# Layer one of two expert layers behind attention: 512-token first products beside attention, their results parked in DRAM, instead of 256-token products of both kinds with partial sums

## The chip, the cores and the metric

The kernel runs on one core of a Trainium2 chip. The metric is the device time of one execution in microseconds (us); three executions of the kernel before took 1135.73 to 1136.03, median 1135.93. Five engines work side by side: TensorE (PE in the profile; its weight loads are PEld), VectorE (DVE), ScalarE (ACT), GpSimd (POOL), and SyncE (SP), which here only issues DMA transfers. Each takes its own instructions in a fixed order and waits on semaphores for the others.

## The reference

Attention with a threshold per row, then two dense layers, each a product, a nonlinearity and a second product. All is float32.

```python
# 4 batches, 8 heads, 576 tokens, head size 64
scores = q @ k.T / 8
scores = where(scores >= max(scores) - tau, scores, -1e9)
x = softmax(scores) @ v            # -> x: 2304 tokens x 512
# layer one                         w_in: 512 x 2048, w_out: 2048 x 512
h = x @ w_in
g = where(h >= 1, h, where(h <= -1, 0, (h + 1)**2 / 4))
x2 = g @ w_out
# layer two, other weights
h = x2 @ w_in2
out = (h * clip(h + 3, 0, 6) / 6) @ w_out2
```

## The kernel before

**Dense layers.** Both are computed in a split form: each float32 operand is cut into a high part (type fp32r) and the remainder, and a product is the sum of three matmuls, high times high, high times low and low times high. Tokens lie along the free axis, in four main blocks of 512 (one a batch) and one block of 256 that collects the last 64 tokens of every batch. The 2048 inner columns are cut into 16 strips `f` of 128. `em_h` makes the first product of one strip: 4 slices of the inner 512 times 3 matmuls, 12 in all, into one PSUM bank; then ACT computes Relu and Square of it (L642, L643), DVE the rest of the nonlinearity (L644) into a tile `r`, ACT the high part `gh` (L650) and POOL the low part `gl` (L651). `em_out` adds a strip's second product to four accumulators, again 12 matmuls. The weights come as float64 words and are turned into high and low float32 parts by `split_a` and `split_b`, on ACT, DVE and POOL.

**Attention.** 16 jobs (`jobs`: a batch and a pair of heads), each of five blocks of queries. Per block: scores on PE (L296), negated copy and row minimum on DVE (L309), exponential on ACT (L320), mask and row sum on DVE (L328), turning by PE transposes (L254) that ACT copies out (`Gf`, L352), and the product with v (L388). One job after the other.

**How the two are put together.** While the first four jobs run there is nothing else for PE. From the fourth job on, `dense1` feeds pieces of layer one between the pieces of attention; `share` (0.57) says how much of it for each piece of attention. Its work is planned in `ROUNDS`: groups of 256 tokens (`GRP`) of the first three batches, and of the 16 strips only the first ten (`NF1`). A round makes ten first products (the first two groups in two halves of five), keeps the split results in SBUF, and makes the second products in two halves of the output rows in `em_part`, in one PSUM bank (Q3). The sum over these ten strips is a partial sum; it goes to the DRAM tile `x2p`. The first product has one PSUM bank while attention runs (`H_TAGS` is Q2 alone), the product with v has Q1, the transposes have Q0, and the scores have four banks in two pairs. After attention `dense` does the rest: batch 3 and the 256-token block in full, strips 10 to 15 of the first three batches (the partial sums are read back and added, L721), and then layer two.

**What sets the order.** The program is written step by step, but a scheduler places every instruction on its engine by a simulated timeline; `after` and `pin_mlp` add a few constraints. The order of each engine below is read from the built program.

```python
        credit = min(credit + share, 3.0)
        while credit > 0:
            c = next(part1)
            if c is None:
                break
            credit -= c
```

This loop runs once per piece of attention, and `part1` is `dense1`; it gives None when the next group's attention is not done.

## Time and profile before

| | |
|---|---|
| median of three executions | 1135.93 us (1135.73 to 1136.03) |
| span of the profiled execution, first to last instruction | 1136.9 us |
| PE busy | 1108.0 us, 97% of the span |
| DVE, ACT, POOL busy | 575.6, 632.6, 404.3 us (51%, 56%, 36%) |
| granted TensorE clock, mean | 0.997 |
| moved by DMA | 80.09 MB, mean 70 GB/s |

The profiled execution is known by its span alone, which is 0.97 us above the median of the three. Attention begins at the start of the span; the first dense matmul on PE starts at 108.7 us, the last of attention ends at 492.4 us. From there to the end PE does only dense work. Matmuls overlap in the pipeline, so that what one of them costs is the distance from its start to the next one's, and not its own duration. One float32 matmul of the program (scores, product with v) stands as two instructions in the trace.

### The profile page before, as it was taken

What the parts mean: (1) busy time and instruction counts of PE and PEld (TensorE: products, weight loads), DVE (VectorE), ACT (ScalarE), POOL (GpSimd) and SP (SyncE); (2) the same over time, 40 slices, a digit from 0 to 9 for tenths busy, and PEclk for the clock granted to TensorE, in tenths of its full rate; (3) what the DMA queues carried; (4) which work ended last, traced back from release to release, by engine and by line L of the source; (5) the groups of instructions that cost most, each with busy time, mean ns of one, the idle gap of its engine ahead of it and who ended that gap; (6) DMA issues with size and microseconds to landing.
All of it is one profiled execution on the core that took longest, in us unless ns stands there. A gap on an engine that the chain in (4) does not pass through costs nothing.

```text
span 1136.9 us, 18024 instructions
## 1 busy us (share of the span) xinstructions
PE 1108.0 (97%) x6680; PEld 901.2 (79%) x6680; DVE 575.6 (51%) x1272; ACT 632.6 (56%) x1239; POOL 404.3 (36%) x383
## 2 busy tenths in 40 slices
PE   7998899999999999999999999999999999999998
PEld 5665567778777788788889988888888888898886
DVE  5888887766565565445545756557511111121111
ACT  5787987866666666556566766645432222333222
POOL 0222676411111111136645765557622222222221
PEclk8999999999999999999999999999999999999999
DMA  6434335222111210015322344533110110010001
GB/s 161 106 77 102 109 108 151 63 81 71 47 49 32 53 43 13 11 34 167 98 75 93 117 143 150 184 111 111 38 42 1 32 38 1 10 38 1 19 1 38
DMA packets 105368, 80.09 MB, mean 70 GB/s; under 512 B 66368, under 2 KB 90176, under 8 KB 105280
## 3 DMA queue, kind: packets, MB, share of 16 engines
q1 hardware_dynamic: 103920, 78.64, 23.9%
q8 instruction: 53, 0.87, 0.3%
q10 hardware_dynamic: 1360, 0.30, 0.1%
q14 instruction: 35, 0.29, 0.1%
HBM read 61.60 MB, written 17.30 MB: 69 GB/s over the span
## 4 chain that ended last, share of the span: by engine, by line
PE 88%; ACT 4%; DVE 4%; issue 1%; DMA 1%; POOL 1%; ACTq 0%; SPq 0%; DVEq 0%
PE Q L633 34%; PE P L675 27%; PE Q L695 7%; PE P L296 7%; PE Q L388 6%; PE Q L254 5%; DVE p L309 2%; ACT e L320 1%; PE P L254 1%; DVE p L328 1%; ACT Gf L352 1%; PE P L426 0%; POOL w_c L135 0%; DMA w_raw<-in_moe_w_in_dram 0%; DVE xl L617 0%
## 5 line engine op out<-in xcount | busy, mean ns | idle before, releaser
L651 POOL TENSOR_TENSOR gl<-r,gh 128x512 fp32r<-128x512 f32 (+1 forms) x190 | 203.3, 1071 | 548.4 <-ACT gh L650 547.9
L633 PE MATMUL Q<-xh,wih 128*128 128x512 f32 (+1 forms) x760 | 263.2, 346 | 2.5 <-DVE r L644 2.5
L633 PE MATMUL Q<-xh,wil 128*128 128x512 f32 (+1 forms) x760 | 257.0, 338 | 0.0
L633 PE MATMUL Q<-xl,wih 128*128 128x512 f32 (+1 forms) x760 | 256.8, 338 | 0.0
L647 DVE SCALAR_TENSOR_TENSOR r<-r,Q 128x512 f32<-128x512 f32 (+1 forms) x80 | 50.7, 634 | 249.0 <-ACT r L646 248.9
L650 ACT ACTIVATE gh<-r 128x512 fp32r<-128x512 f32 (+1 forms) x190 | 99.8, 526 | 126.2 <-PE P L675 53.3
L633 PEld LDWEIGHTS Q<-xh,wih 128*128 128x128 f32 x760 | 143.9, 189 | 25.0 <-issue 4.8
L633 PEld LDWEIGHTS Q<-xl,wih 128*128 128x128 f32 x760 | 143.9, 189 | 15.7
L633 PEld LDWEIGHTS Q<-xh,wil 128*128 128x128 f32 x760 | 143.8, 189 | 15.2
L646 ACT ACTIVATE r<-Q,three 128x512 f32<-128x512 f32 (+1 forms) x80 | 51.4, 643 | 143.7 <-PE Q L633 140.6
L309 DVE TENSOR_SCALAR_CACHE_REDUCE p<-P 128x576 f32<-128x576 f32 x144 | 104.3, 754 | 50.2 <-PE Q L254 32.0
L328 DVE SCALAR_TENSOR_TENSOR p<-p,th,e 128x576 f32<-128x576 f32 x144 | 121.3, 860 | 15.7 <-ACT e L320 14.9
L644 DVE SCALAR_TENSOR_TENSOR r<-r,Q 128x256 f32<-128x256 f32 (+1 forms) x110 | 55.0, 500 | 135.1 <-ACT r L643 127.7
L320 ACT ACTIVATE e<-p,nm 128x576 f32<-128x576 f32 x144 | 109.1, 774 | 25.4 <-DVE p L309 24.3
L254 PE MATMUL Q<-ident,p 128*128 128x128 f32 x656 | 109.8, 283 | 11.3 <-ACT Gf L352 4.9
L675 PE MATMUL P<-woh,gh 128*128 128x512 f32 x288 | 112.0, 390 | 0.6 <-DVE ob L733 0.6
L675 PE MATMUL P<-wol,gh 128*128 128x512 f32 x288 | 112.3, 390 | 0.0
L254 PEld LDWEIGHTS Q<-ident,p 128*128 128x128 f32 x656 | 74.5, 141 | 46.3 <-ACT Gf L352 12.7
L675 PE MATMUL P<-woh,gl 128*128 128x512 f32 x288 | 111.0, 390 | 0.0
L296 PE MATMUL P<-kt,qt 64*128 64x288 f32 (+1 forms) x640 | 100.5, 433 | 6.0 <-DVE p L309 4.9
L135 POOL TENSOR_TENSOR w_c<-w_c,w_raw 128x512 int32<-128x512 int32 x64 | 88.6, 1384 | 39.1 <-DVE w_c L133 22.7
L352 ACT ACTIVATE Gf<-Q 128x512 f32<-128x512 f32 x128 | 74.9, 594 | 40.0 <-PE Q L254 39.2
(84 smaller groups left out, 1865.1 us busy)
## 6 DMA issues: line engine op xcount, KB each, us to landing
w_raw<-in_moe_w_in_dram SPq DMA_DIRECT2D x32, 512.0 KB, 4.1
w_raw<-in_moe_w_out_dram SPq DMA_DIRECT2D x32, 512.0 KB, 3.7
kn<-in_k_dram SPq DMA_DIRECT2D x32, 128.0 KB, 2.6
vn<-in_v_dram SPq DMA_DIRECT2D x32, 128.0 KB, 2.9
x2p<-ob SPq DMA_DIRECT2D x16, 256.0 KB, 2.2
x2d<-ob SPq DMA_DIRECT2D x16, 256.0 KB, 4.1
xst<-x2d SPq DMA_DIRECT2D x16, 256.0 KB, 3.3
out_dram<-ob SPq DMA_DIRECT2D x16, 256.0 KB, 2.2
```

Source lines behind the costliest of these rows:

```text
L135: x = G.tensor_tensor(out=c.bitcast(I32), in0=c.bitcast(I32), in1=r, op=ALU.add)
L254: x = T.transpose(out, in_, ident)
L296: mm = T.matmul(o, qt[j][r, c], kt[j][r, k0:k0 + HS], start=True, stop=True, skip_group_check=True)
L309: reads(V.tensor_scalar(out=p[:, x], in0=s[:, :, 0:HS], scalar1=-1.0, scalar2=3e38, op0=ALU.mult, op1=ALU.min, accum_out=nm[:, x:x + 1]), ...
L320: pins["S"] = S.activation(out=e, in_=p[:, x], func=ACTF.Exp, bias=nm[:, x:x + 1], scale=-1.0)
L328: V.scalar_tensor_tensor(out=p[:, x], in0=p[:, x], scalar=th[:, x:x + 1], in1=e, op0=ALU.is_le, op1=ALU.mult, accum_out=zt[j][:, z:z + 1])
L352: S.activation(out=f[:, h, :, d0:d0 + 128], in_=tm.rearrange("p (c n) -> p c n", c=4), func=ACTF.Copy)
L633: mm = T.matmul(h, l[:, kk * 128:(kk + 1) * 128], r, start=(x == 0), stop=(x == 3 * KD - 1))
L650: x = S.activation(out=gh, in_=r, func=ACTF.Copy)
L651: y = G.tensor_tensor(out=gl, in0=r, in1=f32(gh), op=ALU.subtract)
L675: T.matmul(a, l, r, start=(first and x == 0), stop=(last and x == 2))
L695: mm = T.matmul(o, l, r, start=(f == fs[0] and x == 0 and i == 0), stop=(f == fs[-1] and x == 2 and i == 1), skip_group_check=True)
```

## The change

Beside attention only first products are made, on 512 tokens at once, for all 16 strips of the first three batches (48 steps of `em_h`). The result `r` is not split there: it goes to DRAM (`gd`, one tile for each block and strip). The function `second` later reads it back with `load_g`, splits it (`split_g`; for odd strips of layer one DVE makes the low part in POOL's place), and makes the second products of a block over all 16 strips in one go, so that partial sums, `x2p`, `em_part`, `ROUNDS` and the rows of `dense` that add partial sums go away. The first products of batch 3 and of the 256-token block run between the second products of the first two blocks. All 16 strips of `w_in` and four of `w_out` are prepared beside attention (before: ten of each). The transposes of attention get a second PSUM bank, Q3, by turns with Q0. `share` is 0.27.

```diff
-    GRP = 256
-    NG = (NB - 1) * MAIN // GRP
-    NF1 = 10
+    NO = 4
...
+    wide = {"g": ctx.enter_context(tc.tile_pool(name="g2", bufs=1))}
+    gd = [[dram.tile([128, n], F32, name=f"gd{w}_{f}") for f in range(KF)] for w, n in enumerate(WIDE)]
...
-        tm = bank("Q0" if mode["mlp"] or mode["n"] % 2 else "Q2")
+        tm = bank("Q0" if mode["n"] % 2 else "Q3" if mode["mlp"] else "Q2")
...
+    def split_g(m, g, f, r):
+        n = WIDE[g]
+        gh = wide["g"].tile([128, n], F32R, tag="gh", name="gh", bufs=MLAG + 1)
+        gl = wide["g"].tile([128, n], F32R, tag="gl", name="gl", bufs=MLAG + 1)
+        x = S.activation(out=gh, in_=r, func=ACTF.Copy)
+        if m == 0 and f % 2:
+            V.tensor_tensor(out=gl, in0=r, in1=f32(gh), op=ALU.subtract)
+        else:
+            pins["G"] = G.tensor_tensor(out=gl, in0=r, in1=f32(gh), op=ALU.subtract)
+        pins["S"] = x
+        gs[m, g, f] = (gh, gl)
...
-        hp_, hb = (mt, HOLD) if key[2] == 1 else (wide["g"], MLAG + 1)
-        r = hp_.tile([128, n], F32, tag="r", name="r", bufs=2)
+        r = (wide["x"] if m else mt).tile([128, n], F32, tag="r", name="r", bufs=2 if m else 3)
         if m == 0:
             S.activation(out=r, in_=h, func=ACTF.Relu, scale=0.5, bias=half)
             S.activation(out=r, in_=r, func=ACTF.Square)
-            vlast = V.scalar_tensor_tensor(out=r, in0=r, scalar=1.0, in1=h, op0=ALU.min, op1=ALU.max)
+            V.scalar_tensor_tensor(out=r, in0=r, scalar=1.0, in1=h, op0=ALU.min, op1=ALU.max)
+            nc.sync.dma_start(out=gd[g][f], in_=r)
...
+    def load_g(g, f):
+        r = wide["g"].tile([128, WIDE[g]], F32, tag="gin", name="gin", bufs=3)
+        nc.sync.dma_start(out=r, in_=gd[g][f])
+        split_g(0, g, f, r)
...
-    def em_part(key, half, f):
-        gh, gl = gs[key, f] if half == 0 else gs.pop((key, f))
...
-    def dense1(ready, ahead):
-        for n, l in enumerate(steps[:n_h]):
...
-            for i, (r, half, f) in enumerate(l):
-                if i == 1:
-                    pace(n + 0.5)
-                yield from em_part(round_key(r), half, f)
-                yield 0.33
+    def dense1(ahead):
+        for n, (g, f) in enumerate((g, f) for g in range(NB - 1) for f in range(KF)):
+            if (0, g) not in xs:
+                while not ready(g):
                     yield None
+                split_x(0, g)
+            ahead(n)
+            if g == NB - 2 and f in (KF - 4, KF - 3):
+                load_g(0, f - KF + 4)
+            yield from em_h(0, g, f)
...
+    def second(seq, hseq, ahead):
+        for n, (g, f) in enumerate(seq):
+            if n + MLAG < len(seq):
+                load_g(*seq[n + MLAG])
+            ahead(n)
+            for i in range(KD):
+                em_out(0, g, f, i, fin_whole)
+            if n < len(hseq):
+                hg, hf = hseq[n]
+                split_x(0, hg)
...
+                for _ in em_h(0, hg, hf):
                     pass
...
-    weights.items += [(kind, 0, f) for kind, f in by_use]
+    weights.add(0, range(KF), "i")
+    weights.add(0, range(NO), "o")
...
-    share = 0.57
+    share = 0.27
     FIRST, RATE = 5, 0.85
...
-    order3 = [NB - 1, *range(NB - 2), NB, NB - 2]
-    dense(0, 2, seq2, fin_whole, ahead2, [(1, order3[0], 3)], rest)
+    FIRST_B = [g for g in range(NB + 1)]
+    seq = [(g, f) for g in FIRST_B for f in range(KF)]
+    hseq = [(g, f) for g in (NB - 1, NB) for f in range(KF)]
+    second(seq, hseq, ahead2)
+    dense2([*range(NB - 1), NB, NB - 1], ahead3)
```

In the built program the matmuls of 256 tokens fall from 2016 to 576, and those of 512 rise from 2448 to 3168.

PE in the middle of attention, from the end of one first product to the start of the next (P are score banks, Q_ with a transpose's `ident` the turning of `p`). Before:

```order
L633 MATMUL Q_3425<-xh,wil_1094 128x256
L296 MATMUL P_3517<-kt,qt 128x288
...
L254 MATMUL Q_3441<-ident,p 128x128 x4
L695 MATMUL Q_3477<-gh,woh_2387 128x256
...
L695 MATMUL Q_3477<-gh,wol_2484 128x256
L254 MATMUL Q_3486<-ident,p 128x128
L633 MATMUL Q_3501<-xh,wih_1344 128x256
```

And after, at a place that fifteen of the 48 steps resemble:

```order
L630 MATMUL Q_3600<-xh,wih_2163 128x512
...
L630 MATMUL Q_3600<-xh,wil_2164 128x512
L249 MATMUL Q_3719<-ident,p 128x128 x4
L291 MATMUL P_3728<-kt,qt 128x288
...
L249 MATMUL Q_3755<-ident,p 128x128
L249 MATMUL Q_3762<-ident,p 128x128 x4
L630 MATMUL Q_3689<-xh,wih_2226 128x512
```

The twelve matmuls of a second product that stood between the two first products are gone; nine transposes and four score matmuls are left there.

ACT at the same places (L642 and L638 are the Relu, L643 and L639 the Square of the first product). Before:

```order
L642 ACTIVATE r<-Q_3425,half 128x256
L643 ACTIVATE r<-r 128x256
L650 ACTIVATE gh<-r 128x256
L352 ACTIVATE Gf<-Q_3441 128x4x128
L320 ACTIVATE e<-p,nm 128x576
```

After:

```order
L638 ACTIVATE r<-Q_3600,half 128x512
L347 ACTIVATE Gf<-Q_3719 128x4x128
L639 ACTIVATE r<-r 128x512
L363 ACTIVATE Gt<-Q_3755 128x128
L347 ACTIVATE Gf<-Q_3762 128x4x128
L315 ACTIVATE e<-p,nm 128x576 x2
```

The copy of the high part has gone from here, and a copy of transposes stands between Relu and Square.

SP at the first steps of the dense work (`vn`, `qn`, `kn` are attention's inputs, `w_raw` the weights). Before:

```order
L434 DMA xd_76<-xu 128x512
L438 DMA xd_80<-xu 128x64
L97 DMA w_raw<-in_moe_w_out_dram 128x1024
L241 DMA vn_96<-in_v_dram 128x4x64 x2
L242 DMA vn_96<-in_v_dram 64x64
L94 DMA w_raw<-in_moe_w_in_dram 128x4x256
```

After:

```order
L431 DMA xd_79<-xu 128x512
L435 DMA xd_83<-xu 128x64
L89 DMA w_raw<-in_moe_w_in_dram 128x4x256
L641 DMA gd_0_89<-r 128x512
L650 DMA gin<-gd_0_89 128x512
L236 DMA vn_174<-in_v_dram 128x4x64 x2
L237 DMA vn_174<-in_v_dram 64x64
L89 DMA w_raw<-in_moe_w_in_dram 128x4x256
```

The store of a strip and, for the first six strips, its reading back stand ahead of loads of attention and of weights.

## Rows read from the trace of the kernel before

**Rows 1.** The page: busy time of engines, PE and clock in 40 slices, bytes.
```profile
PE 1108.0 (97%) x6680; PEld 901.2 (79%) x6680; DVE 575.6 (51%) x1272; ACT 632.6 (56%) x1239; POOL 404.3 (36%) x383
PE   7998899999999999999999999999999999999998
PEclk8999999999999999999999999999999999999999
GB/s 161 106 77 102 109 108 151 63 81 71 47 49 32 53 43 13 11 34 167 98 75 93 117 143 150 184 111 111 38 42 1 32 38 1 10 38 1 19 1 38
```

**Rows 2.** Stretches: us, busy time of each engine (instructions), clock, DMA share, GB/s.
```profile
20.00:120.00 100.00, 92.87 (x686) 60.87 (x686) 87.81 (x261) 82.53 (x171) 22.63 (x28) 1.00 0.40 107
124.00:200.00 76.00, 69.42 (x516) 52.77 (x516) 63.22 (x146) 62.04 (x135) 54.06 (x52) 1.00 0.48 135
200.00:260.00 60.00, 58.28 (x456) 47.37 (x455) 41.25 (x116) 45.75 (x98) 17.31 (x21) 1.00 0.25 67
260.00:487.00 227.00, 223.93 (x1747) 181.03 (x1746) 127.94 (x379) 144.10 (x314) 30.68 (x48) 1.00 0.16 41
...
700.00:725.00 25.00, 25.00 (x112) 20.72 (x111) 16.02 (x22) 15.68 (x27) 14.87 (x12) 1.00 0.56 177
```

**Rows 3.** The chain that ended last, by time: start us, us, what.
```profile
79.03 2.31 PE Q L388 x20
...
99.74 2.31 PE Q L388 x20
...
260.75 2.84 PE Q L388 x20
...
292.71 2.84 PE Q L388 x20
...
515.07 7.19 PE Q L695 x60
...
545.41 2.72 PE Q L633 x12
```

**Rows 4.** Groups of PE instructions by shape: count, busy us, mean ns, idle before, releasers.
```profile
L633 PE MATMUL Q<-xh,wih 128*128 128x256 f32 x368 | 110.4, 300 | 2.5 <-DVE r L644 2.5
L254 PE MATMUL Q<-ident,p 128*128 128x128 f32 x656 | 109.8, 283 | 11.3 <-ACT Gf L352 4.9 <-DVE p L328 3.2 <-ACT Gt L366 2.3
L695 PE MATMUL Q<-gh,woh 128*128 128x256 f32 x240 | 74.6, 311 | 0.5 <-ACT ob L706 0.5
```

**Rows 5.** Timeline, one hand-over of the first product's bank: start us, us, what.
```profile
342.99 0.28 PE L633 MATMUL Q<-xh,wil 128*128 128x256 f32 x1
...
343.37 0.47 ACT L642 ACTIVATE r<-Q,half 128x256 f32<-128x256 f32 x1 [0.19 <-PE Q L633]
...
343.88 0.42 ACT L643 ACTIVATE r<-r 128x256 f32<-128x256 f32 x1
...
344.40 0.42 DVE L644 SCALAR_TENSOR_TENSOR r<-r,Q 128x256 f32<-128x256 f32 x1 [2.67 <-ACT r L643]
```

**Rows 6.** Timeline, the same hand-over early, where it held PE.
```profile
137.99 0.28 PE L633 MATMUL Q<-xh,wil 128*128 128x256 f32 x1
...
143.25 0.41 DVE L644 SCALAR_TENSOR_TENSOR r<-r,Q 128x256 f32<-128x256 f32 x1
...
143.71 0.39 PE L633 MATMUL Q<-xh,wih 128*128 128x256 f32 x1 [0.41 <-DVE r L644]
```

**Rows 7.** Groups of the same steps at 512 tokens, and of copies, by shape.
```profile
L642 ACT ACTIVATE r<-Q,half 128x512 f32<-128x512 f32 x34 | 23.0, 680 | 8.8 <-POOL gl L651 3.4 <-PE Q L633 2.7 <-DMA x2p<-ob 2.3
L643 ACT ACTIVATE r<-r 128x512 f32<-128x512 f32 x34 | 21.2, 627 | 0.5
L644 DVE SCALAR_TENSOR_TENSOR r<-r,Q 128x512 f32<-128x512 f32 x34 | 23.2, 686 | 67.2 <-ACT r L643 60.8 <-DMA xst<-xd 6.4
L650 ACT ACTIVATE gh<-r 128x512 fp32r<-128x512 f32 x98 | 61.7, 631 | 92.8 <-PE P L675 47.7 <-DVE r L647 35.4 <-DVE r L644 9.6
L651 POOL TENSOR_TENSOR gl<-r,gh 128x512 fp32r<-128x512 f32 x98 | 130.6, 1333 | 270.4 <-ACT gh L650 270.1
L352 ACT ACTIVATE Gf<-Q 128x512 f32<-128x512 f32 x128 | 74.9, 594 | 40.0 <-PE Q L254 39.2
```

**Rows 8.** Timeline: five transposes and eight score instructions on PE.
```profile
334.04 0.71 PE L254 MATMUL P<-ident,qn 128*128 128x128 f32 x5
...
334.68 1.19 PE L296 MATMUL P<-kt,qt 64*64 64x288 f32 x8
```

**Rows 9.** DMA issues: out<-in, count, KB each, median us to landing.
```profile
x2p<-ob SPq DMA_DIRECT2D x16, 256.0 KB, 2.2
...
xst<-x2d SPq DMA_DIRECT2D x16, 256.0 KB, 3.3
...
pb<-x2p SPq DMA_DIRECT2D x12, 256.0 KB, 4.4
```

More of the change, by code (lines that the diff above doesn't have):

```diff
@@ L811, in dense, with dense2 @@
+    def dense2(order, ahead):
+        seq = [(g, f) for g in order for f in range(KF)]
         for n, (g, f) in enumerate(seq):
-            key = (m, g, ph)
-            split_x(key)
-            ahead(n, g, f)
-            for c in em_h(key, m, f):
-                pass
-            if rest is not None:
-                rest(n)
-            if m == 0 and g < NB - 1 and f == fs[g][-3]:
-                load_part(g)
-            kk = fs[g].index(f) + KD + 1 - len(fs[g])
+            split_x(1, g)
+            ahead(n)
+            for _ in em_h(1, g, f):
+                pass
+            kk = f + KD + 1 - KF
@@ L968, in ahead3 @@
-    def ahead3(n, g, f):
+    H_TAGS[:] = ["Q0", "Q1", "Q2", "Q3"]
+    wide["wo"] = ctx.enter_context(tc.tile_pool(name="wext", bufs=1))
+    wide["late"] = ctx.enter_context(tc.tile_pool(name="late", bufs=1))
+    weights.add(0, range(NO, KF), "o")
+    for c in part1:
+        weights.half()
+    weights.add(1, range(KF), "i")
+    weights.add(1, range(KF), "o")
+    split_x(0, NB - 1)
+    FIRST_B = [g for g in range(NB + 1)]
+    seq = [(g, f) for g in FIRST_B for f in range(KF)]
+    hseq = [(g, f) for g in (NB - 1, NB) for f in range(KF)]
@@ new lines, in enter_second, with ahead2, ahead3 @@
+    def enter_second():
+        mt_es.close()
+        wide["x"] = ctx.enter_context(tc.tile_pool(name="xs2", bufs=1, side="right"))
+    def ahead2(n):
+        limit = 2 * KF
+        if n >= KF:
+            limit += min(n - KF, KF)
+        if n < KF:
+            weights.upto(KF + n + 1)
+        for _ in range(2):
+            if weights.done < limit:
+                weights.half()
+        if n == len(seq) - 2:
+            split_x(1, 0)
+    second(seq, hseq, ahead2)
+    def ahead3(n):
```

278 lines of the change are left out of this document (71 added, 207 removed).

## The prediction

> **What bounds the kernel now.** The page comes first: PE is busy 97% of the span and the granted clock is at full speed in all slices but the first [rows 1]. Then the stretches, because one share for a whole program hides where an engine waits. From 260 to 487 us, attention with dense work beside it, PE is busy 223.93 of 227 us, while DVE has 56% and ACT 63%; from 700 to 725 us, dense work alone, PE has all 25 us [rows 2]. The losses are early: 6.6 us of 76 from 124 to 200 us and 1.7 of 60 after that, where POOL is busy 71% of the time with weights and DVE and ACT are over 80% [rows 2]. Before the dense work begins (20 to 120 us) DVE has 88% and sets the pace. So the kernel is PE's issue rate plus some 11 us of waiting beside attention (6.6, 1.7 and 3.1), and a change is worth what it takes off PE's sequence, less what it makes PE wait.
>
> How much a matmul costs is read from the chain: 60 matmuls of 256 tokens take 7.19 us, 119.8 ns each, and 12 of 512 tokens take 2.72 us, 226.7 ns each [rows 3]. Two of the narrow ones cost 239.6, so a pair costs 12.9 ns more than one wide one. A job of attention without dense work takes 20.7 us (from 79.03 to 99.74), one with it 32.0 (260.75 to 292.71) [rows 3]; 114 narrow matmuls of dense work stand in such a job, 13.7 us, so attention itself needs 18.3 us of PE.
>
> **The change, part by part.**
>
> *Fewer, wider matmuls.* Of the 1104 narrow first-product matmuls (three forms of 368, [rows 4]) 384 belong to the 256-token block and stay; 720 go, and so do all 720 of the narrow second products (three forms of 240). They are 1440 x 119.8 = 172.6 us. In their place stand 720 wide ones, 720 x 226.7 = 163.2 us. PE is the path in both places, so the saving counts in full: **-9.4 us**. The Trainium skill has a rule against this: "TensorE: Matmul & The Clock Gate", Part 1, gives a warm start-to-start of N / 2.4 GHz plus about 2.5 ns, which would be 109.2 and 215.8 ns, and the saving 1.9 us by it. The rows measure more fixed time than that for each of these matmuls, and the sum goes by the rows.
>
> *Work moved out from under attention.* Beside attention PE had 1321 narrow matmuls, 158 us; now it has 576 wide ones, 131 us. The rest runs later, where PE is already full, so this moves time and doesn't add any, provided that the shorter stretch is still PE's. Its 363 us (124 to 487) become about 336. DVE was busy 232 us there and ACT 252 [rows 2]. DVE's dense part stays nearly the same (58 x 0.42 us of L644 and some 25 us of splits and copies against 48 x 0.69 and fewer splits [rows 5, 7]); ACT loses about 18 us, since the high part of the result isn't made there any more. That gives DVE 69% and ACT 70% of the new stretch. They have room on the mean; what they cost is latency.
>
> *The hand-over of the first product's bank.* Beside attention this product still has the one bank Q2: the next may start only when DVE's last step has read it. At 256 tokens this took 1.83 us from the start of the last matmul (342.99) to the end of L644 (344.82) where nothing was in the way [rows 5]. At 512 the Relu is 0.21 longer, the Square 0.21, DVE's step 0.27 [rows 7], and the last matmul 0.11: 2.63 us, or 2.41 behind the matmul's own slot. The second product's 12 matmuls, which stood between two first ones and covered this, are gone. In the built order fifteen of the 48 hand-overs have too little PE work between: typically nine transposes and four scores, 9 x 0.11 + 1.19 + some switching = 2.3 us [rows 8]. And at most of these ACT has a copy of transposes (0.594, [rows 7]) or a like piece between Relu and Square. Adding, for each place, 2.41 plus what ACT's order has between, less PE's work between, the fifteen shortfalls sum to 9.6 us (0.2 to 1.0 each). The same sum over the old order is 4.4 us, and PE really waited 2.5 [rows 4]. Scaled like that the new wait is 5.5, in full it is 9.6; net of the 2.5 it is 3.0 to 7.1. I take the middle: **+5.0 us**.
>
> *A second bank for the transposes.* PE waited 4.9 us for copies of `Gf` and 2.3 for `Gt` [rows 4], all with one bank where dense work ran. With two by turns part of that goes. Also POOL makes no low parts beside attention, and weights come in a slower succession (15 items over some 18 longer steps), in the very stretch that lost 8.3 us. Bounds 0 and -8; I take **-3.0 us**, near the waits named in that stretch's rows.
>
> *A pause.* Three blocks of 16 steps use up attention's batches just as they finish. Once, before the third block, some 14 us of attention's PE work stands alone in the order. Alone, attention runs at 20.7 us a job where PE needs 18.3 [rows 3]: 14 x 2.4 / 18.3 = **+1.8 us**.
>
> *DRAM.* Sixty-four stores and loads of 256 KB and sixteen of 128 KB come, 32 transfers of partial sums go; at the densest that is 256 KB for 2.72 us of PE, 94 GB/s, where slices of 184 GB/s stand in the page [rows 1]. A load lands in 3.3 to 4.4 us [rows 9]; with 0.63 for the high and 1.33 for the low part [rows 7] that is 6.4 us, against two steps (5.4 us) by which `second` asks ahead, and three buffers that let SP issue earlier. On SP a strip's store waits for DVE, and the first six readings back wait for their own store to land (2.2 us, [rows 9]); behind them stand loads of `vn`, `qn` and weights, for which unit and weight steps would wait if they were late. These are asked for about a job ahead. Between 0 and +4; I take **+0.5 us**, for the changes of block in the later part too.
>
> *At no cost.* The additions of partial sums (L721) and their loads were hidden beside PE's full stretch. The twelve remaining strips of `w_out` and layer two's weights are prepared in steps of 4.2 to 5.4 us, under engines that had 60% of the time beside the same PE rate [rows 2].
>
> *Sum.* -9.4 + 5.0 - 3.0 + 1.8 + 0.5 = -5.1 us on a span of 1136.9: 1131.8. The median lies 0.97 below that span, so **1130.8 us**, 0.45% less.
>
> **The rivals.** A measurement of this kernel can tell about 0.2%, 2.3 us, from no change.
>
> *Even.* The hand-overs cost their full 7.1, the transposes' bank gives nothing back since DVE and ACT set their copies' time: -9.4 + 7.1 + 1.8 + 0.5 = 0, 1135.9. For it: ACT's order puts a copy into nearly each short place. Against it: the old order, read the same way, waited only 57% of what it showed.
>
> *Slower: the hand-over is late everywhere.* Early chains were far longer than the undisturbed one: 5.67 us from the last matmul to the end of L644 at 137.99, and PE held by it [rows 6]. Fifteen such chains from 111 to 202 us average 3.9 us. If the first 16 steps have this plus 0.8, their shortfalls sum to 14.7; the later ones, with 0.6 more than undisturbed, 5.5. Net of 2.5: -9.4 + 17.7 + 1.8 + 0.5 = +10.6, 1146.5. It decides from the point where waits of the first product for DVE's last step exceed some 14 us. Against it: those early chains were made by weights and POOL at 71%, both thinner now.
>
> *Slower: the round trip is on the path.* If each load is issued only two steps ahead and never earlier, 48 steps without first products lose up to 0.4 us each: +19 on the rest, 1150. Against it: three buffers, and a slot that is free long before.
>
> *Much faster.* The early 8 us go nearly whole and the hand-overs cost 1: -9.4 + 1 - 8 + 1.8 + 0.5 = -14.1, 1121.8.
>
> *The quoted rule.* With 1.9 in place of 9.4 saved, the rest as forecast: +2.4, 1138.3. The chain's rows speak against it.
>
> **How the numbers follow.** Forecast (its own range 1127 to 1134) 0.50; even 0.18; hand-over late 0.12; round trip 0.03; much faster 0.14; the rule 0.03. Faster by more than 0.2% (under 1133.7): 0.48 of the forecast and the much faster case, 0.62. Within: even and the forecast's edge, 0.20. Slower: 0.18. The range from 1122 to 1140 leaves out the two slow mechanisms and the edge of the fast one.
>
> **What would show it.** Right: twelve wide matmuls in 2.72 us everywhere; waits of the first product for DVE's last step of 5 to 10 us in all, at fifteen or so places, nearly all under 1 us; attention's last PE work near 468 us in place of 492; PE full from there on. Wrong: gaps on PE behind `gin` or `gl` after attention; jobs beside dense work at much over 30 us; waits for `qn`, `kn` or weights; or a wide matmul that costs more than 227 ns while stores to DRAM run.

## The result and the profile after

The changed kernel takes **1153.41 us** (median of 4 runs, 1151.0 to 1154.1) where the kernel before took 1135.98 beside it: ratio 1.0148, 95% interval 1.0134 to 1.0163. That is 1.5% slower; the forecast was 1130.8, 0.45% faster. The profiled execution took 1154.1 us, its span is 1152.3, so 15.4 us more than the span before.

The page of the changed kernel, answering to [rows 1]: busy time, PE and clock in 40 slices, bytes. A slice is 28.8 us.

```profile
PE 1109.4 (96%) x5960; PEld 862.5 (75%) x5960; DVE 568.0 (49%) x1234; ACT 606.5 (53%) x1117; POOL 351.6 (31%) x313
...
PE   7999998989999999999998899999999999999998
...
PEclk9999999989999999999999999999999999999999
...
DMA packets 118691, 105.43 MB, mean 91 GB/s; under 512 B 68176, under 2 KB 90192, under 8 KB 118608
```

PE has 720 matmuls fewer and is still busy for the same 1109 us, against 1108.0. The recorded end of a matmul is modelled and a wide one is longer, so this line alone doesn't say whether time was saved. The slices say where it went. Between its first and its last slice the kernel before has 8s for PE from 85 to 142 us only; the changed one has them at 173 to 202, at 230 to 259 and from 605 to 662 us, and PEclk has an 8 at 230 to 259.

Stretches of the changed kernel, answering to [rows 2]: us, busy time of each engine (instructions), clock, DMA share, GB/s.

```profile
124.00:200.00 76.00, 69.45 (x420) 46.63 (x422) 56.71 (x140) 59.80 (x116) 33.42 (x33) 1.00 0.49 146
200.00:260.00 60.00, 54.45 (x297) 37.19 (x295) 46.08 (x113) 43.02 (x82) 22.67 (x21) 0.91 0.34 101
260.00:470.00 210.00, 205.71 (x1267) 145.95 (x1264) 125.65 (x359) 133.45 (x255) 5.87 (x14) 1.00 0.23 69
625.00:650.00 25.00, 16.97 (x65) 12.86 (x64) 17.45 (x25) 15.07 (x31) 15.62 (x12) 0.86 0.71 231
700.00:725.00 25.00, 25.00 (x112) 20.68 (x112) 2.83 (x5) 5.47 (x9) 5.91 (x5) 1.00 0.27 80
```

Three things are to be seen. From 124 to 200 us PE waits as long as before (6.55 against 6.58), although POOL is busy 44% instead of 71%. From 200 to 260 it now waits 5.55 (1.72 before), at a mean granted clock of 0.91. And from 625 to 650 us, long after attention, PE has only 16.97 of 25 us at a clock of 0.86, while DVE is busy 70%. At 700 PE is full, and DVE, ACT and POOL have next to nothing to do: the work that was there before (DVE 16.02, POOL 14.87 of 25 us, [rows 2]) has been done earlier.

The chain of waits, answering to the last two lines of [rows 3]: start, us, what.

```profile
493.19 2.72 PE Q L630 x12
495.91 2.72 PE P L679 x12
```

PE's groups by shape, answering to [rows 4]: count, busy us, mean ns, idle before, releasers.

```profile
L630 PE MATMUL Q<-xh,wih 128*128 128x512 f32 x512 | 206.4, 403 | 4.4 <-DVE r L640 4.1 <-ACT xh L601 0.2
...
L679 PE MATMUL P<-wol,gh 128*128 128x512 f32 x288 | 112.5, 391 | 2.1 <-POOL wol L134 2.1
...
L249 PE MATMUL Q<-ident,p 128*128 128x128 f32 x656 | 103.9, 282 | 10.3 <-DVE p L323 5.4 <-ACT Gf L347 3.1 <-ACT Gt L363 0.9
...
L679 PE MATMUL Q<-gh,woh 128*128 128x512 f32 x64 | 21.2, 413 | 8.2 <-DVE r L640 5.5 <-ACT gh L613 2.7
```

The saving is there: 12 wide matmuls take 2.72 us, 226.7 ns each, while stores and loads run. The wait for the hand-over of bank Q2 beside attention is small: 4.1 us, where I had expected 5 to 10. The new waits are the last row's 8.2 us, one of them 5.5 us long, and 2.1 us for weights of layer two.

**Where 15.4 us went.** For every kernel below I read from all PE records when attention's last PE work ends, and take off attention's own PE work (16 jobs, my estimate of 293.8 us, the same for all, so that only differences between kernels count) and the dense matmuls issued by then at 119.8 or 226.7 ns. What is left is the *loss beside attention*, the start included; the same from there to the end of the span is the *loss behind*. *Waits* are the time without any PE record, from 106 us to attention's end and from there on; the last column is the time at which the clock records show half speed (1.2 of 2.4 GHz), to the end of dense work, with "(at 12)" or "(at 88)" where it lies before the dense work. From the two prices as printed the loss behind comes out 0.3 to 0.5 us higher in every row; its differences hold to 0.2 us.

| kernel | median us | span | attention's end | loss beside | loss behind | waits beside / behind | half clock, us |
|---|---|---|---|---|---|---|---|
| before | 1135.98 | 1136.9 | 492.4 | 40.3 | 5.8 | 14.6 / 0.6 | 6.8 (at 12) |
| changed | 1153.41 | 1152.3 | 475.3 | 49.3 | 21.7 | 16.9 / 11.4 | 3.4 + 6.8, 6.8 behind |
| e1_late_w2 | 1150.11 | 1148.2 | 476.8 | 50.9 | 16.1 | 16.9 / 7.2 | 3.4 (at 12), 3.4 + 3.4 + 6.8 |
| e2_gin_late | 1152.56 | 1145.7 | 469.9 | 44.0 | 20.4 | 16.0 / 10.5 | 6.8 behind |
| e5_late_gin | 1148.40 | 1143.0 | 470.5 | 44.5 | 17.2 | 15.2 / 8.0 | 3.4 |
| e6_no_w2 | 1139.15 | 1136.3 | 473.1 | 47.2 | 7.9 | 16.4 / 1.8 | 3.4 + 3.4 |
| e10_low_on_dve | 1149.27 | 1150.5 | 476.5 | 50.5 | 18.7 | 17.9 / 7.6 | 3.4 (at 12), 3.4 + 6.8, 6.8 behind |
| e11_late_low_on_dve | 1142.64 | 1140.5 | 473.9 | 47.9 | 11.2 | 16.0 / 3.9 | 3.4 (at 88), 3.4 + 3.4 |
| e13_five_strips | 1130.02 | 1126.2 | 463.9 | 37.9 | 7.0 | 10.7 / 1.5 | none |
| e14_before_five_strips | 1131.24 | 1129.7 | 485.8 | 33.8 | 5.3 | 7.4 / 0.6 | 3.4 (at 88) |

The changed kernel against the one before: -9.4 for the matmuls, +9.0 beside attention (forecast +3.8), +15.9 behind it (forecast +0.5); sum +15.5. That this meets the spans' difference follows from how the losses are made and is no test of the -9.4.

**What stops PE at 626.9.** The timeline of the changed kernel; weight-load rows and other rows that aren't needed are left out. L119, L122 and L128 are DVE's three steps of a weight strip, L130 POOL's first; L111 and L118 are ACT's steps of a strip, L613 is ACT's high part of a result read back and L617 POOL's low part of one; L638 is the Relu of the first product, L639 its Square and L640 DVE's last step of it.

```profile
626.65 0.28 PE L630 MATMUL Q<-xh,wil 128*128 128x256 f32 x1
627.08 0.67 ACT L118 ACTIVATE w_c<-w_raw 128x512 f32<-128x512 f32 x1 [0.42 <-DMA w_raw<-in_moe_w_in_dram]
...
627.44 0.41 DVE L122 TENSOR_SCALAR w_c<-w_c 128x512 uint32<-128x512 uint32 x1
...
627.65 0.61 ACT L613 ACTIVATE gh<-gin 128x512 fp32r<-128x512 f32 x1
627.89 0.69 DVE L128 SCALAR_TENSOR_TENSOR w_c<-w_raw,w_c 128x512 uint32<-128x512 uint32 x1
628.17 0.66 ACT L111 ACTIVATE w_raw<-w_raw 128x512 int32<-128x512 uint32 x1
628.50 0.42 DVE L119 TENSOR_SCALAR w_c<-w_c 128x512 f32<-128x512 f32 x1
628.72 1.34 POOL L130 TENSOR_TENSOR w_c<-w_c,w_raw 128x512 int32<-128x512 int32 x1 [1.81 <-issue]
628.73 0.45 ACT L638 ACTIVATE r<-Q,half 128x256 f32<-128x256 f32 x1
628.95 1.39 DVE L122 TENSOR_SCALAR w_c<-w_c 128x512 uint32<-128x512 uint32 x1
629.22 0.42 ACT L639 ACTIVATE r<-r 128x256 f32<-128x256 f32 x1
630.02 1.45 POOL L617 TENSOR_TENSOR gl<-gin,gh 128x512 fp32r<-128x512 f32 x1
...
630.38 1.64 DVE L128 SCALAR_TENSOR_TENSOR w_c<-w_raw,w_c 128x512 uint32<-128x512 uint32 x1
...
631.94 0.41 DVE L640 SCALAR_TENSOR_TENSOR r<-r,Q 128x256 f32<-128x256 f32 x1
...
632.40 0.80 PE L679 MATMUL Q<-gh,woh 128*128 128x512 f32 x1 [5.47 <-DVE r L640]
```

PE has finished a narrow first product and comes to the next block of the second one, whose sums stand in banks Q0 to Q3. One of these is still to be read by L640. ACT is late first: it does L118, L613 and L111 before the Relu, which starts 1.80 us after PE's last matmul has ended (626.93). The Square ends at 629.64, and L640 starts 2.30 us later. In between stands DVE, which does steps of two weight strips first, 0.41, 0.69, 0.42, 1.39 and 1.64 us, and the last two take over twice what the same steps take at 627: each lies beside a POOL instruction. L640 itself, beside POOL too, takes its usual 0.41. PE waits 5.47 us, and towards the end of the wait the clock falls, to 1.2 GHz for 6.8 us from 631.4 on: 0.86 is the mean of this stretch.

### The profile page after: what moved, and what is told of

Its sections match the earlier page's. It is cut to its first block, busy times and chain, and to the rows that moved or that the text cites. A ratio compares the mean times of both kernels' runs of the same rounds, so it can differ in the third digit from the quotient of the medians.

```text
span 1152.3 us, 16662 instructions
## 1 busy us (share of the span) xinstructions
PE 1109.4 (96%) x5960; PEld 862.5 (75%) x5960; DVE 568.0 (49%) x1234; ACT 606.5 (53%) x1117; POOL 351.6 (31%) x313
## 4 chain that ended last, share of the span: by engine, by line
PE 74%; DVE 9%; ACT 6%; issue 4%; DMA 3%; POOL 3%; SPq 0%; ACTq 0%; POOLq 0%; DVEq 0%
PE Q L630 31%; PE P L679 23%; PE Q L385 6%; PE P L291 5%; PE Q L679 4%; PE Q L249 4%; DVE p L304 2%; DVE w_c L128 2%; DVE p L323 2%; DVE w_c L122 1%; POOL w_c L130 1%; DMA gin<-gd 1%; DMA gd<-r 1%; DVE w_c L119 1%; ACT e L315 1%
## 5 line engine op out<-in xcount | busy, mean ns | idle before, releaser
L630 PE MATMUL Q<-xh,wih 128*128 128x512 f32 (+1 forms) x640 | 242.5, 379 | 4.4 <-DVE r L640 4.1
L630 PE MATMUL Q<-xl,wih 128*128 128x512 f32 (+1 forms) x640 | 237.4, 371 | 0.0
L630 PE MATMUL Q<-xh,wil 128*128 128x512 f32 (+1 forms) x640 | 237.4, 371 | 0.0
L644 DVE SCALAR_TENSOR_TENSOR r<-r,Q 128x512 f32<-128x512 f32 (+1 forms) x80 | 50.7, 635 | 260.4 <-ACT r L643 260.3
L617 POOL TENSOR_TENSOR gl<-r,gh 128x512 fp32r<-128x512 f32 (+1 forms) x80 | 96.5, 1207 | 240.2 <-ACT gh L613 239.3
L630 PEld LDWEIGHTS Q<-xh,wih 128*128 128x128 f32 x640 | 121.5, 190 | 34.8 <-DVE r L640 9.0
L630 PEld LDWEIGHTS Q<-xl,wih 128*128 128x128 f32 x640 | 121.7, 190 | 21.3 <-DVE p L304 0.5
L630 PEld LDWEIGHTS Q<-xh,wil 128*128 128x128 f32 x640 | 121.3, 190 | 21.3
L643 ACT ACTIVATE r<-Q,three 128x512 f32<-128x512 f32 (+1 forms) x80 | 51.4, 644 | 149.2 <-PE Q L630 143.7
L323 DVE SCALAR_TENSOR_TENSOR p<-p,th,e 128x576 f32<-128x576 f32 x144 | 120.2, 859 | 9.3 <-ACT e L315 8.3
L304 DVE TENSOR_SCALAR_CACHE_REDUCE p<-P 128x576 f32<-128x576 f32 x144 | 104.5, 753 | 30.0 <-PE P L291 29.4
L249 PE MATMUL Q<-ident,p 128*128 128x128 f32 x656 | 103.9, 282 | 10.3 <-DVE p L323 5.4
L130 POOL TENSOR_TENSOR w_c<-w_c,w_raw 128x512 int32<-128x512 int32 x64 | 91.7, 1434 | 71.8 <-DVE w_c L128 31.0
L291 PE MATMUL P<-kt,qt 64*128 64x288 f32 (+1 forms) x640 | 98.8, 427 | 10.2 <-DVE p L304 7.0
L640 DVE SCALAR_TENSOR_TENSOR r<-r,Q 128x512 f32<-128x512 f32 (+1 forms) x80 | 50.4, 631 | 110.5 <-ACT r L639 110.4
L638 ACT ACTIVATE r<-Q,half 128x512 f32<-128x512 f32 (+1 forms) x80 | 51.1, 639 | 73.4 <-PE Q L630 73.2
L613 ACT ACTIVATE gh<-gin 128x512 fp32r<-128x512 f32 (+1 forms) x80 | 46.7, 585 | 73.3 <-PE P L679 37.5
```

The source lines that it names most:

```text
L130: x = G.tensor_tensor(out=c.bitcast(I32), in0=c.bitcast(I32), in1=r, op=ALU.add)
L249: x = T.transpose(out, in_, ident)
L291: mm = T.matmul(o, qt[j][r, c], kt[j][r, k0:k0 + HS], start=True, stop=True, skip_group_check=True)
L304: reads(V.tensor_scalar(out=p[:, x], in0=s[:, :, 0:HS], scalar1=-1.0, scalar2=3e38, op0=ALU.mult, op1=ALU.min, accum_out=nm[:, x:x + 1]), ...
L323: V.scalar_tensor_tensor(out=p[:, x], in0=p[:, x], scalar=th[:, x:x + 1], in1=e, op0=ALU.is_le, op1=ALU.mult, accum_out=zt[j][:, z:z + 1])
L617: pins["G"] = G.tensor_tensor(out=gl, in0=r, in1=f32(gh), op=ALU.subtract)
```

## The experiments

All run beside the kernel before, whose median was 1137.1 for e1 to e4, 1136.55 for e5 to e8, 1136.93 for e10 to e12 and 1137.3 for e13 to e15. Experiments e1 to e4 came first: two moves of work, two banks.

**e1_late_w2.** Layer two's first strips later and at half the pace:
```
-        if n >= KF:
-            limit += min(n - KF, KF)
+        if n >= 2 * KF:
+            limit += min((n - 2 * KF) // 2 + 1, KF)
```


> The changed kernel with layer two's 16 strips of w_in prepared one for every two steps from step 32 of the second products on, in place of one a step in steps 16 to 31 (beside the 256-token block). Theory W (those weights, on DVE and POOL in short steps, hold DVE's last step of the first products, and that holds PE at 632 us for 5.5 us, then in half clock): the wait at about 632 us and the half clock behind it go, the stretch after attention shrinks from 677 to about 664 us, the time from 1153 to about 1141. Theory D (the reading back from DRAM is late, whatever the weights do): the waits stay, 1150 or more. The stretch up to the end of attention stays at 475 us in both.

1150.11 us, ratio 1.0112 (1.0097 to 1.0127); loss behind 16.1 in place of 21.7. Waits of PE from 600 us on, in all and the longest:

```profile
PE Q L679 <- DVE gl L615: 2.7, 4, 1.4
PE P L679 <- POOL wol L134: 2.1, 2, 1.7
PE Q L679 <- ACT gh L613: 0.9, 1, 0.9
```

The wait of 5.5 us is gone, with the dip of the clock behind it; smaller ones for `gl` came in its place, since the strips now run beside steps of 2.72 us. The move takes back 5.6 of the 15.9 us that the loss behind had grown by, and 3.3 us of the median, where 12 were expected.

**e2_gin_late.** The first six readings back wait for the store of strip 11 of the third block:
```
-            nc.sync.dma_start(out=gd[g][f], in_=r)
+            x = nc.sync.dma_start(out=gd[g][f], in_=r)
+            if (g, f) == (NB - 2, KF - 5):
+                pins["D"] = x
...
-        nc.sync.dma_start(out=r, in_=gd[g][f])
+        x = nc.sync.dma_start(out=r, in_=gd[g][f])
+        after(x, pins["D"])
```


> The changed kernel with the first readings back held behind the store of strip 11 of the third block on SP, so that none stands between attention's loads early. Theory S (six readings back that wait on SP for their own store, 9 us of SP's time from 100 to 300 us, and their splits make the early dense stretch slow): attention ends 4 to 6 us before 475, the time falls to about 1148. Theory H (what is lost beside attention comes from the longer hand-over of the first product and from DVE slowed beside POOL, not from SP): attention ends at 474 to 476 and the time stays within 2 us of the changed kernel.

1152.56 us (1147.44 to 1154.74), ratio 1.0145 (1.0128 to 1.0162). The profiled execution is the fastest of its four; in it attention ends at 469.9 and no dip of the clock lies beside attention. Over all runs the gain can't be told from none. Together with e1 (e5) it may be 1.7 us.

**e3_two_h_banks.** Two banks for the first product beside attention, and one for the transposes as in the kernel before:
```
-        tm = bank("Q0" if mode["n"] % 2 else "Q3" if mode["mlp"] else "Q2")
+        tm = bank("Q0" if mode["mlp"] or mode["n"] % 2 else "Q2")
...
-    H_TAGS = ["Q2"]
+    H_TAGS = ["Q2", "Q3"]
```


> The changed kernel with two banks for the first product beside attention (Q2 and Q3), and one for attention's transposes as before the change. Theory Q (the single bank's longer hand-over is a main loss beside attention): waits of the first product for DVE's last step (4.1 us directly) go, attention ends 4 to 8 us before 475, and the time is about 1147. Theory H2 (DVE standing in its own order for that last step, 83 us of idle time from 100 to 475, is the loss, and a second bank doesn't shorten that): little changes, or the lost second bank of the transposes costs up to 3 us.

1176.64 us, ratio 1.0350 (1.0335 to 1.0366). PE's transposes by shape in it:

```profile
L249 PE MATMUL Q<-ident,p 128*128 128x128 f32 x656 | 111.0, 285 | 26.0 <-ACT Gf L347 18.1 <-DVE p L323 3.2 <-ACT Gf L350 2.5
```

The transposes wait 26.0 us in place of 10.3. So a second bank for the product, at this price, isn't what the changed kernel lacks beside attention. The exchange of the bank costs 23 us, but not by the bank alone: the scheduler also put 604 of the 3744 dense matmuls at other places among attention's.

**e4_p_banks.** The sums of the block that follows the narrow first products stand in P banks, so that L640 no longer holds them:
```
-            if m == 0 and g % 2 == 0 and g >= NB - 2:
+            if m == 0 and g == NB:
```


> The changed kernel with the accumulators of the third block's second product in the two score pairs (P) and not in the first products' four banks. Theory B (the 5.5 us wait is only the clash over these banks; the rest of the work is in time): the wait at 632 goes, the half clock with it, and the time is 8 to 11 us less, about 1143. Theory W (DVE, POOL and ACT are behind by then, whichever bank is used): PE stops nearby for the split of a strip read back (gh, gl), and the gain is under 4 us.

1160.06 us, ratio 1.0206 (1.0188 to 1.0223). Waits of PE from 600 us on:

```profile
PE P L679 <- DVE ob L690: 8.5, 2, 7.8
PE P L679 <- ACT ob L688: 4.2, 4, 2.1
```

The P banks were held as well: L690 and L688 copy out the sums of the block before, and L690 stands in the same late queue of DVE. Which bank PE meets decides where it waits; this run doesn't show a free one.

**e5_late_gin.** Both edits of e1 and e2.

> The changed kernel with two edits together: layer two's first strips are prepared at half the pace from the 33rd step of the second product on, and the first six readings back wait for the store of strip 11 of the third block. Theory W+S (layer two's strips beside the short steps cost DVE its time, about 6 us of the 16 by this edit; readings back in front of the loads on SP cost some 5 us beside attention): the two add, span 1141 to 1144, attention's last PE work near 470, loss behind it near 16. Rival R (each is only where the same late work shows, so that one takes what the other gave): no better than the first edit alone, 1148 to 1150.

1148.40 us (1141.7 to 1151.44), ratio 1.0094 (1.0068 to 1.012). The profiled span, 1143.0, is as expected, but three of six runs lie at 1151, and the median is the rival's: the gain beside attention doesn't hold in all runs. The runs at 1151 have a mean granted clock of 0.993 to 0.994, the faster three 0.998 to 1.000.

**e6_no_w2.** Layer two's strips left out; layer two takes layer one's:
```
-    weights.add(1, range(KF), "i")
-    weights.add(1, range(KF), "o")
...
-        wh, wl = wsp["i", m, f]
+        wh, wl = wsp["i", 0, f]
...
-        wh, wl = wsp["o", m, f]
+        wh, wl = wsp["o", 0, f]
```


> The changed kernel with nothing of layer two's weights loaded or prepared: layer two multiplies by layer one's split weights. So 32 strips of ACT, DVE and POOL work and 16.8 MB of loads are left out, and PE's work is the same. Theory W (the strips are what makes DVE late behind attention): the loss behind attention falls from 21.7 to 6 to 8 us, no wait of PE for DVE's last step at 632, no half clock there; span 1137 to 1139. Rival D (the round trip through DRAM, and the steps that ask only two ahead, cost it by themselves): the waits for gh and gin stay, the loss stays over 14, span over 1145. Beside attention nothing changes by either: its last PE work near 475.

1139.15 us (11 runs), ratio 1.0021 (1.001 to 1.0033), and loss behind 7.9. The stretch of it that answers to 625:650 above:

```profile
625.00:650.00 25.00, 23.74 (x103) 18.97 (x103) 10.40 (x14) 11.38 (x21) 5.34 (x4) 1.00 0.64 199
```

PE has 23.74 in place of 16.97 us at the full clock, with the same stores and loads of results. So 14.3 of the 17.4 us lost are the strips of layer two; the round trip by itself isn't it. Their loads go here together with their preparation, and no run leaves out the one without the other. That it is the preparation which holds PE at 626.9 is read from the timeline above.

**e7_spread_wo.** The four `w_out` strips beside attention spread out:
```
-        goal = min(2 * len(weights.items), 2 * FIRST + 2 * RATE * n)
+        goal = min(2 * len(weights.items), 2 * FIRST + 2 * RATE * n, 2 * KF + max(0, (n - 14) // 3))
```


> The changed kernel with the four strips of w_out beside attention spread: half a strip in three steps instead of 1.7 halves in each, since nothing needs them before attention ends. Theory B (two strips at once made DVE late for the softmax at 248 us, 2.13 us, and the clock fell behind it): no wait over 1.5 us and no half clock from 235 to 260, attention ends 3 to 6 us earlier, near 470; median near 1149. Rival (the strips are in any case too few, what is late is DVE behind ACT's Square): attention ends within 2 us of 475 and a dip of the clock comes elsewhere; median within 2 us of 1153.

1153.01 us, ratio 1.0144 (1.0129 to 1.0159). The dip from 249 us is gone from its profile, another stands at 181, and attention's end isn't earlier (476.4; by then 12 more dense matmuls are done, and the loss beside is 47.7). A miss: these four strips are at most a small part of what costs.

**e8_all_moved.** e5, e7, and three of layer two's `w_out` strips from the 66th step on:
```
+        if n >= 4 * KF + 2:
+            limit += (n - 4 * KF - 2) // 5 + 1
```


> All moves of work together: late readings back, w_out's strips spread beside attention, layer two's w_in at half the pace from the 33rd step, and three of layer two's w_out strips from the 66th step on (they are what layer two's second product waits for at 791 and 801). If the losses are those that the traces name, and they add: loss beside attention near the forecast's (attention ends near 468), behind it near 13, span 1136 to 1139, about the kernel before. If each move only makes other work late: 1146 to 1150.

1148.62 us, ratio 1.0097 (1.0084 to 1.011): no better than e5, so moving strips about gained nothing more.

**e10_low_on_dve.** POOL's low parts of strips and of layer one's results, behind attention, on DVE:
```
-        if m == 0 and f % 2:
+        if m == 0:
             V.tensor_tensor(out=gl, in0=r, in1=f32(gh), op=ALU.subtract)
...
-        x = G.tensor_tensor(out=lo, in0=f32(c), in1=f32(hi), op=ALU.subtract)
+        x = (G if mode["att"] else V).tensor_tensor(out=lo, in0=f32(c), in1=f32(hi), op=ALU.subtract)
```


> The changed kernel with POOL's two low parts behind attention given to DVE: that of the result read back (gl, every second one was on POOL) and that of a weight strip (L134). POOL keeps one piece a strip (L130). DVE then has some 70 pieces more. Theory P (DVE is late because each of its pieces that runs beside a POOL piece takes 1.4 to 1.8 us where it takes 0.42 to 0.69 alone, so the strips hurt by POOL and not by their number): DVE's L119, L122, L128, L615 fall to means under 0.75, the loss behind attention falls from 21.7 to 12 or less though DVE has more to do; median 1141 to 1146. Rival N (DVE has simply too many pieces and waits in its order): 70 pieces of 0.69 more, 48 us, make it worse; loss over 22, median 1154 or more.

1149.27 us, ratio 1.0111 (1.0096 to 1.0125). DVE's groups from 470 to 800 us in it; the same lines in the changed kernel have means of 685 (L119), 968 (L122) and 1062 ns (L128).

```profile
L615 DVE TENSOR_TENSOR gl<-gin,gh 128x512 fp32r<-128x512 f32 (+1 forms) x77 | 59.9, 780 | 74.7 <-ACT gh L613 74.6
L128 DVE SCALAR_TENSOR_TENSOR w_c<-w_raw,w_c 128x512 uint32<-128x512 uint32 x36 | 36.7, 1021 | 0.4
L119 DVE TENSOR_SCALAR w_c<-w_c 128x512 f32<-128x512 f32 x36 | 21.4, 594 | 1.8 <-ACT w_c L118 1.2
L122 DVE TENSOR_SCALAR w_c<-w_c 128x512 uint32<-128x512 uint32 x36 | 19.5, 543 | 0.8
```

DVE has some 75 pieces more and PE waits less for it (7.6 us behind attention in place of 11.4), so the rival is out. But the time fell by 4 us and not by 7 to 12: L128 stays slow beside L130, which POOL kept, L615 has a mean of 780 ns where it had 697, and another wait came at the block's turn. ACT's order in e10 there:

```profile
633.36 0.58 ACT L688 ACTIVATE ob<-P 128x512 f32<-128x512 f32 x1
639.69 0.63 ACT L601 ACTIVATE xh<-xst 128x512 fp32r<-128x512 f32 x1 [5.75 <-DMA xst<-x2d]
640.23 0.61 ACT L613 ACTIVATE gh<-gin 128x512 fp32r<-128x512 f32 x1
```

The high part of layer two's `x`, which waits for its load, stands ahead of `gh`, for which PE waits 4.2 us.

**e11_late_low_on_dve.** e5 and e10 together.

> The same two low parts on DVE behind attention, and the two moves of e5 (layer two's first strips at half the pace from the 33rd step, readings back later). Theory P with W: loss behind attention 7 to 9 us, attention's last PE work near 470, span 1133 to 1137, so within 0.2% of the kernel before or a little under it. Rival N: over 1148.

1142.64 us, ratio 1.0054 (1.0041 to 1.0067). Loss behind 11.2, against 17.2 in e5: with the strips later, the low parts on DVE are worth 6 us. The expected 7 to 9 wasn't reached.

**e12_all_low_on_dve.** The strips' low part on DVE beside attention as well.

> As the one before, with the strips' low part on DVE beside attention too, where DVE is busy 83% of the time. Theory P: a POOL piece of 1.3 to 1.7 us that slows DVE's pieces for its whole length goes for one DVE piece of 0.69; the waits of 2.4 and 2.1 us at 180 and 245 us shrink below 1 and attention ends near 467, 2 to 4 us earlier than in the one before. Rival N (DVE's share is the bound there): attention ends later, over 473, with more waits for p and r.

1142.8 us (1139.52 to 1146.29), ratio 1.0047 (1.0032 to 1.0062); attention's end 471.5 against 473.9. In the median nothing; inconclusive. It is, with e11, the best whole version of the changed kernel, and doesn't reach the kernel before.

What was still open then was whether the loss beside attention is the change's own or the strips' too.

**e13_five_strips, e14_before_five_strips.** Both kernels with only five strips prepared, ahead of the dense work, and each later dense matmul on one of the five (the edit is that of the changed kernel):
```
+        def of(self, f):
+            return wsp[self.items[f % max(1, min(FIVE, self.done))]]
...
-        wh, wl = wsp["i", m, f]
+        wh, wl = weights.of(f)
...
-    weights.add(0, range(KF), "i")
-    weights.add(0, range(NO), "o")
+    weights.add(0, range(FIVE), "i")
...
```


> The changed kernel in which only the first five strips of w_in are prepared, before the dense work begins; every later matmul takes one of these five, so that 59 strips of loads and of ACT, DVE and POOL work are left out and PE's order is the same. To be read against the kernel before with the same left out. Theory V (the change itself is sound, its saving of 9.4 less some 4 for hand-over and pause; all above that is strips that collide): loss beside attention near 40, behind it near 6, no half clock, span 1126 to 1131 and 3 to 6 us under the kernel before without strips. Rival H (the one bank's hand-over and attention's order cost the saving): loss beside attention stays over 45, and it is no faster than the other.

> The kernel before with the same left out: five strips prepared, 59 not, every later matmul takes one of the five. Theory V: the early waits (6.6 us from 124 to 200) go in part, the rest of PE's time was full already: span 1129 to 1135. Rival H: the same here; it differs in what the changed kernel does beside it.

1130.02 us (0.9939 of the kernel before, 0.9925 to 0.9952) and 1131.24 (0.9946, 0.9933 to 0.9959). PE's order was to stay the same and did so for the most part: 314 of 3744 dense matmuls in e13 and 216 of 4464 in e14 stand at another place among attention's. Without strips the kernels differ by 1.2 us, which these runs can't tell from nothing, where with them they differ by 17. Stretches of e13, then of e14:

```profile
124.00:200.00 76.00, 73.16 (x440) 48.88 (x441) 42.89 (x122) 47.79 (x89) 2.84 (x5) 1.00 0.30 89
200.00:260.00 60.00, 57.84 (x363) 40.06 (x362) 40.44 (x115) 40.03 (x77) 1.99 (x4) 1.00 0.26 76
260.00:460.00 200.00, 194.88 (x1187) 138.47 (x1186) 118.61 (x338) 126.02 (x239) 5.83 (x14) 1.00 0.22 65
625.00:650.00 25.00, 25.00 (x112) 20.66 (x111) 8.77 (x12) 9.21 (x16) 6.08 (x5) 1.00 0.55 176
```

```profile
124.00:200.00 76.00, 74.36 (x549) 56.20 (x548) 45.99 (x136) 49.93 (x111) 10.81 (x16) 1.00 0.20 53
200.00:260.00 60.00, 59.46 (x462) 47.38 (x461) 36.30 (x107) 39.42 (x85) 8.19 (x13) 1.00 0.25 70
260.00:460.00 200.00, 197.05 (x1535) 158.25 (x1534) 119.05 (x353) 129.60 (x279) 26.82 (x41) 1.00 0.16 41
```

In e13 PE is full from 625 to 650 us with 176 GB/s of traffic. Beside attention it still waits more than in e14, 1.2, 1.6 and 2.2 us in the three stretches, and that is what the change's own order costs: loss beside 37.9 against 33.8, 4.1 us. Behind, 7.0 against 5.3. The spans differ by 3.5 us (1126.2 and 1129.7). But these two profiles are the fastest run of e13 and the slowest of e14, and e14's has 3.4 us of half clock at 88 us; the medians leave 1.2.

**e15_before_low_on_dve.** The kernel before with the strips' low part on DVE everywhere.

> The kernel before with the strips' low part (POOL, 1.3 us and more, and DVE's pieces slowed beside it) on DVE everywhere. Theory P: as in the changed kernel, DVE's pieces get shorter in the early stretch and part of the 6.6 us of waits there goes: median 1132 to 1135. Rival N (DVE at 83% is the bound there): 1137 to 1142.

1144.42 us, ratio 1.0065 (1.0052 to 1.0078): slower. From 124 to 200 us in it:

```profile
124.00:200.00 76.00, 68.65 (x497) 51.73 (x494) 64.05 (x147) 59.31 (x130) 34.85 (x37) 0.98 0.44 125
```

POOL has 34.85 us in place of 54.06, and PE still waits 7.35 (6.58 before). Beside attention the loss grows by 3.2 us, where DVE is the busiest engine, and behind it by 2.5. So here the longer queue of DVE costs more than the freer POOL gives.

## Why the prediction was wrong

*The step that failed: "At no cost".* I put the preparation of layer two's weights at nothing, "in steps of 4.2 to 5.4 us, under engines that had 60% of the time beside the same PE rate". With their loads they cost 14 us (e6). The share of [rows 2] at 700 us was true, and PE was full there, with a first and a second product of 512 tokens to each step, 5.4 us. In the changed kernel `ahead2` puts one strip in each 4.16 us step (12 wide and 12 narrow matmuls), up to the place where a block ends and PE has nothing else next in its order. A mean share of 70% tells nothing about one step that stands behind two strips in DVE's queue. And I gave no length to a strip's steps where they stand in a queue. Nearly two strips in the 5.47 us wait take 4.55 us; alone they would take 2.63 (0.41, 0.69, 0.42, 0.42, 0.69), so their lengthening is worth at most some 1.9 us there, and ACT's late Relu 1.8. Long steps by themselves hold nothing up: in the kernel before they stand in the stretch of [rows 2] from 700 us too, where PE is full and has other products next in its order.

```profile
704.38 1.40 DVE L127 TENSOR_SCALAR w_c<-w_c 128x512 uint32<-128x512 uint32 x1
...
705.81 1.66 DVE L133 SCALAR_TENSOR_TENSOR w_c<-w_raw,w_c 128x512 uint32<-128x512 uint32 x1
```

My list of signs looked for gaps behind `gin` or `gl`. Gaps behind attention came, but the longest stood behind `r`, the first product's hand-over, for which I had a term beside attention only.

*-9.4 for the matmuls* held: 2.72 us for twelve wide ones at the full clock. By the rule that I quoted from the Trainium skill ("TensorE: Matmul & The Clock Gate", Part 1) the saving would have been 1.9. The trace doesn't agree: the medians from start to start are 227 and 120 ns in both kernels.

*+5.0 - 3.0 + 1.8 beside attention*, 3.8 in all, is 4.1 without strips (e13 against e14, in these two profiles). That the sum came so near is luck, for its parts were off. The hand-over's wait is 2.4 us there (1.0 in e14) and 4.1 in the changed kernel (2.5 before): 1.4 to 1.6 more, and not 5.0. The second bank of the transposes, which I put at -3 with a bound of -8, costs 23 us when it goes to the first product (e3); how much of that is the bank and how much the other order is not shown. I had read its worth from the waits that one bank made in the kernel before. The thinner POOL, my other reason for the -3, gave nothing from 124 to 200 us (6.55 against 6.58). No run shows the pause by itself. And the whole, forecast at -5.1, is -3.5 without strips by the two profiles and -1.2 by the medians.

*With the strips* the loss beside attention is 9.0 more than before, and not 3.8. Of the 11.4 us between the changed kernel and e13, 6.2 are waits and 5.1 the half clock (10.2 us at half speed); in the kernel before the strips cost 6.5 there (40.3 against 33.8). One such place of the changed kernel, on the timeline:

```profile
244.87 1.41 POOL L130 TENSOR_TENSOR w_c<-w_c,w_raw 128x512 int32<-128x512 int32 x1 [0.62 <-DVE w_c L128]
...
245.15 1.67 DVE L128 SCALAR_TENSOR_TENSOR w_c<-w_raw,w_c 128x512 uint32<-128x512 uint32 x1
...
246.86 0.76 DVE L304 TENSOR_SCALAR_CACHE_REDUCE p<-P 128x576 f32<-128x576 f32 x1
...
248.36 1.13 PE L291 MATMUL P<-kt,qt 64*128 64x288 f32 x6 [2.13 <-DVE p L304]
```

The scores wait 2.13 us for a softmax step behind a strip's step of 1.67, and the dip of the clock follows. The number of strips is the same as before, 20 by attention's end. Why the same strips make PE wait less in the kernel before is argued only: there the second product stands between two first ones and fills such holes. No run puts it back alone.

*+0.5 for DRAM and changes of block* is 1.7 without strips. The readings back that wait on SP (9.2 us of SP's time from 100 to 300 us) cost at most 2 us in the medians (e2, e5), and more in single runs only.

*Of the rivals* none had this mechanism. "The round trip is on the path" gave 1150 and was nearest in time, by the wrong wait: e6 keeps the round trip and has a loss behind of 7.9 us in place of 21.7. "The hand-over is late everywhere" gave 1146.5 and asked for waits over 14 us; they are 4.1.

What stays open: which of the clock's dips beside attention come in which run (e2 and e5 spread over 7 and 10 us), what the loads of the strips cost without their preparation, and the 2 us between the spans and the medians of e13 and e14.

## What to carry to other kernels

Work that is "hidden beside PE" has a price that depends on what stands next to it: when a change moves it, read which single step of which queue PE waits for at the place where it lands, and price the pieces as they last beside their new neighbours, not alone. To know what a change is worth in itself, take the suspected companion out of both kernels and compare: here 17 us became 1. And a resource that shows small waits today (the transposes' one bank) may be worth more after the change than its waits say.

## What the hardware showed

DVE's pieces lengthen beside POOL's by what they read, not by DVE's load. In the changed kernel L128 (two inputs from SBUF) takes 0.69 us alone and up to 1.81 beside POOL, L323 0.82 and up to 1.95, L119 and L122 (one input, SBUF to SBUF) 0.42 and up to 1.57. L640 and L304, which read PSUM, take 0.69 and 0.75 with POOL busy all the time or not at all. The Trainium skill states this in "SBUF — State Buffer", section "Who interferes with whom": a DVE instruction with two SBUF inputs, or in a mode with two ports, contends with GpSimd for a shared pair of ports, one with a single SBUF input outside these modes doesn't. The trace agrees, with the numbers above. Whether L119 and L122 run in such a mode the trace doesn't say; that they lengthen fits it. Of the modes with two ports the page also says that whoever issues first has the shared pair for the whole instruction and the other is blocked. The L122 that starts at 628.95 fits: it ends 0.28 us after POOL's piece (628.72 and 1.34 us long), less than it takes alone. The L128 at 630.38 does alike: it ends 0.55 us after POOL's piece (630.02 and 1.45 us long), so most of it waited. It can also be POOL's piece that is longer: the L130 that starts at 622.53 takes 1.87 us (its mean is 1.43), and the L615 beside it, from 622.55, its usual 0.69.

The opposite move isn't free either. The low parts of strips and results on DVE gained 6 us behind attention (e11 against e5); the strips' low part on DVE lost 7 in the kernel before (e15), over half of it beside attention, where DVE is the busiest engine.

Waits of PE cost more than their length where the clock falls behind them: in the changed kernel 6.8 us at 1.2 GHz begin at 249.1, just behind the wait of 2.13 us that ends at 248, and 6.8 more at 631.4, in that of 5.47 which begins at 627, and none beside the one of 2.43 us that ends at 182. The same place can go either way: the profile of e2, whose PE order is the same, has its 2.12 us wait at 242 without a dip. The profile of the kernel before has none between its start and its end.
